# Program order pinned on every engine in a gated recurrence with a highway layer: gate and product two units ahead, decay one ahead, output one behind

## The chip, the cores and the metric

The kernel runs on one core of one Trainium2 chip. The metric is the device time of one launch in microseconds (us); lower is better. The engines named below: PE is TensorE (matmuls and transposes), DVE is VectorE, ACT is ScalarE, POOL is GpSimd, and SP is the sync engine, whose queue issues the large DMAs. "1024 KB" in a row is 1024 x 1024 bytes, 1.049 MB.

## The reference

For four sequences of 6336 steps and 256 channels a gated linear recurrence runs over time, and a highway layer is applied to its output:

```python
sig = 1 / (1 + exp(-f_logit))
f = lower_bound + (1 - lower_bound) * sig
h[t] = f[t] * h[t-1] + (1 - f[t]) * x[t]          # y[t] = h[t], per sequence and channel
H = maximum(y @ w_h, 0)
T = 1 / (1 + exp(-(y @ w_t + b_t)))
out = T * H + (1 - T) * y
```

Inputs and output are fp32; 1024 rows of 256 values are 1.049 MB.

## The kernel before

The work is cut into 25 units. Unit 0 holds the first 192 steps of all four sequences (768 rows); units 1 to 24 hold 1024 steps of one sequence each, in the order in which the four sequences take turns. The channels are two halves of 128, called h or m. With u = sigmoid(-f_logit) and c = 1 - lower_bound, the decay is f = 1 - c u, and the recurrence is run on b = u x and scaled by c later, so that `ncc` holds -c and the weights and diagonal matrices hold c already.

The steps of one unit, each a helper function of the kernel:

- `load` (line 65): two DMAs on SP's queue bring `lt` (f_logit) and `xt` (x), 128 partitions of eight rows each.
- `gate` (L114): ACT makes `u`, one instruction on the whole unit. `product` (L121): POOL makes `bv` = u x in four instructions.
- `decay_pe` (L128): PE transposes one half of `u`, eight blocks, into the PSUM tile `uT`; `decay_act` (L136): ACT makes the decay `f` from it. `b_pe` (L142): PE transposes one half of `bv` into `bT`.
- `scan` (L153): DVE runs the recurrence over 1024 steps for one half, from `f` and `bT`, into `y`. It starts from the last column of the same sequence, four units earlier.
- `z_pe` (L167), four matmuls into `zp`; `t_act` (L175), ACT's sigmoid `t`. `g_pe` (L181 and L184), six matmuls into `gp`; `d_dve` (L193), DVE's `d`; `e_dve` (L200), DVE's `e` = d t for both halves. z and g of either half need the scans of both halves.
- `o_pe` (L216, L217), called four times with q = 0 to 3: eight matmuls each turn a quarter of the unit back into rows, in `op`; `o_act` (L225): ACT copies the quarter to `o`; after the last quarter one DMA on SP's queue stores the unit (L229).

The PSUM tiles `uT`, `bT`, `zp` and `gp` have one buffer each, `op` has two. In SBUF, `lt` and `xt` have three buffers, `u`, `bv`, `f` and `e` three, `t`, `d` and `o` two, `y` six.

The loop at line 239 emits, in iteration n, steps of units n-2 to n+2: the scan of unit n, z, g, d, t and e of unit n-1, the output of unit n-2, gate, product and decay of unit n+1, and the load of unit n+2. This is the order of the program, but not the order on the engines: a scheduler at build time takes instructions as it expects them to become ready, the program's order being its priority, and fixes a sequence for each engine. At run time each engine and each queue works in that sequence. Buffers are handed on by semaphores: a tile's next user waits until all readers of its buffer are done.

Of the kernel before, what the change touches and what calls it, by code (L numbers as in the profile page):

```python
# [19 lines left out]
def kernel(  # L20
# [19 lines left out]
    P = 128  # L40
# [69 lines left out]

    def gate(n):
        np_, _ = units[n]
        u = mid.tile([P, NB, D], FP16, tag="u")
        nc.scalar.activation(u[:np_], st[n]["lt"][:np_], AF.Sigmoid, scale=-1.0)  # L114
        st[n]["u"] = u

    def product(n):
        np_, _ = units[n]
        bv = mid.tile([P, NB, D], BF16, tag="bv")
        for q in range(0, NB, 2):  # L120
            nc.gpsimd.tensor_mul(bv[:np_, q:q + 2], st[n]["u"][:np_, q:q + 2], st[n]["xt"][:np_, q:q + 2])  # L121
        st[n]["bv"] = bv

    def decay_pe(n, h):
        np_, _ = units[n]
        uT = ps1.tile([P, NB * P], FP16, tag="uT")
        for j in range(NB):
            nc.tensor.transpose(uT[:, j * np_:(j + 1) * np_], st[n]["u"][:np_, j, h * P:(h + 1) * P], ident_h[:np_, :np_])  # L128
        st[n]["uT"] = uT

    def decay_act(n, h):
        np_, _ = units[n]
        N = NB * np_
        if h == 0:
            st[n]["f"] = mid.tile([P, NH, NB * P], FP16, tag="f", name="f")
        nc.scalar.activation(st[n]["f"][:, h, :N], st[n]["uT"][:, :N], AF.Identity, scale=ncc[:, h:h + 1], bias=1.0)  # L136

    def b_pe(n, h):
        np_, _ = units[n]
        bT = ps1.tile([P, NB * P], BF16, tag="bT")  # L140
        for j in range(NB):
            nc.tensor.transpose(bT[:, j * np_:(j + 1) * np_], st[n]["bv"][:np_, j, h * P:(h + 1) * P], ident_b[:np_, :np_])  # L142
        st[n]["bT"] = bT

    carry = {}
# [1 line left out]
    def scan(n, h):  # L147
        if h == 0:
            st[n]["y"] = ypool.tile([P, NH, NB * P], BF16, tag="y", name="y")
        y = st[n]["y"]  # L150
        for b, _, c0, ln in units[n][1]:
            prev = carry.get((b, h))
            nc.vector.tensor_tensor_scan(  # L153
                y[:, h, c0:c0 + ln], st[n]["f"][:, h, c0:c0 + ln], st[n]["bT"][:, c0:c0 + ln],
                0.0 if prev is None else prev, op0=ALU.mult, op1=ALU.add)
            carry[b, h] = y[:, h, c0 + ln - 1:c0 + ln]

    def halves(n):
# [3 lines left out]
    def z_pe(n, m):  # L162
        zp = ps1.tile([P, 2, 512], FP32, tag="zp")
        y = st[n]["y"]
        for ki in range(NH):
            for i, (a, e) in enumerate(halves(n)):
                nc.tensor.matmul(zp[:, i, :e - a], w_sb[:, 1, ki, m * P:(m + 1) * P], y[:, ki, a:e],  # L167
                                 start=ki == 0, stop=ki == NH - 1)
        st[n]["zp"] = zp

    def t_act(n, m):
        w = NB * units[n][0] // 2
        if m == 0:
            st[n]["t"] = ffn.tile([P, NH, 2, 512], BF16, tag="t", name="t")
        nc.scalar.activation(st[n]["t"][:, m, :, :w], st[n]["zp"][:, :, :w], AF.Sigmoid, bias=bt[:, m:m + 1])  # L175

    def g_pe(n, m):
        gp = ps1.tile([P, 2, 512], FP32, tag="gp")
        y = st[n]["y"]
        for i, (a, e) in enumerate(halves(n)):  # L180
            nc.tensor.matmul(gp[:, i, :e - a], ndiag[:, m], y[:, m, a:e], start=True, stop=False)  # L181
        for ki in range(NH):
            for i, (a, e) in enumerate(halves(n)):
                nc.tensor.matmul(gp[:, i, :e - a], w_sb[:, 0, ki, m * P:(m + 1) * P], y[:, ki, a:e],  # L184
                                 start=False, stop=ki == NH - 1)
        st[n]["gp"] = gp

    def d_dve(n, m):
        w = NB * units[n][0] // 2
        if m == 0:  # L190
            st[n]["d"] = ffn.tile([P, NH, 2, 512], BF16, tag="d", name="d")
        y2 = st[n]["y"][:, m, :2 * w].rearrange("p (i w) -> p i w", i=2)
        nc.vector.scalar_tensor_tensor(st[n]["d"][:, m, :, :w], y2, ncc[:, m:m + 1], st[n]["gp"][:, :, :w],  # L193
                                       op0=ALU.mult, op1=ALU.max)

    def e_dve(n):
        w = NB * units[n][0] // 2
        e = mid.tile([P, NH, 2, 512], BF16, tag="e", name="e")
        if w == 512:
            nc.vector.tensor_mul(e, st[n]["d"], st[n]["t"])  # L200
        else:
            for m in range(NH):
                nc.vector.tensor_mul(e[:, m, :, :w], st[n]["d"][:, m, :, :w], st[n]["t"][:, m, :, :w])
        st[n]["e"] = e

    def o_pe(n, q):
        np_, _ = units[n]
        w = NB * np_ // 2
        op = ps2.tile([P, 2, D], FP32, tag="op")
        y, e = st[n]["y"], st[n]["e"]  # L210
        for jj in range(2):
            j = 2 * q + jj
            i, c = divmod(j * np_, w)
            for h in range(NH):
                o = op[:np_, jj, h * P:(h + 1) * P]
                nc.tensor.matmul(o, y[:, h, j * np_:(j + 1) * np_], diag[:, h], start=True, stop=False)  # L216
                nc.tensor.matmul(o, e[:, h, i, c:c + np_], ident_b, start=False, stop=True)  # L217
        st[n]["op"] = op

    def o_act(n, q):  # L220
        np_, segs = units[n]
# [13 lines left out]

    def ok(n):
        return 0 <= n < NU

    for n in range(-2, NU + 2):
        if ok(n + 2) and n + 2 > 1:  # L240
            load(n + 2)
        if ok(n):
            b_pe(n, 0)
            scan(n, 0)
        if ok(n - 1):
            g_pe(n - 1, 0)
# [11 lines left out]
        if ok(n):  # L258
            b_pe(n, 1)
            scan(n, 1)  # L260
        if ok(n + 1):
            decay_pe(n + 1, 0)
            decay_act(n + 1, 0)
        if ok(n - 1):
            g_pe(n - 1, 1)
            z_pe(n - 1, 1)
            d_dve(n - 1, 1)
            t_act(n - 1, 1)
        if ok(n + 1):
            decay_pe(n + 1, 1)  # L270
            decay_act(n + 1, 1)
        if ok(n - 1):
            e_dve(n - 1)
# [37 lines left out]
```

## Time and profile before

| | us |
|---|---|
| median of three runs | 317.29 |
| fastest and slowest of them | 313.27, 318.69 |
| the profiled execution, its whole time | 312.08 |
| its span, first to last instruction | 310.0 |

The rows below come from that one profiled execution, so sums are made against 312.08 and its span. Busy time is what an engine spent in instructions; a chain of waits is followed back from the last instruction to what released it at each step, and its shares are shares of the span. In a timeline row the first number is the start in us from the start of the span, the second the length, then engine, line, operation, tile written from tiles read, and shapes; "xN" merges N instructions of one kind that follow each other. What stands in square brackets is how long the engine had been idle and what ended it. Instructions of one engine may overlap a little at their ends, so the distance from start to start is often shorter than the length shown.

### The profile page before, as it was taken

Reading aid. Unit: us, or ns where it says so; the run is one execution under the profiler, and the core shown is the slowest. Engines: PE = TensorE matmul, PEld = TensorE weight load, DVE = VectorE, ACT = ScalarE, POOL = GpSimd, SP = SyncE. Lnnn points to the kernel's source line nnn. Section 1 sums busy time; section 2 is a strip of 40 time slices with the busy share of each in tenths; the row PEclk is TensorE's granted clock in tenths of the full one; section 3 lists DMA queues with packets and bytes.
Section 4 is the critical chain, followed back from the end, with each engine's and each line's share of the span. In section 5 each row is a group of like instructions: output and inputs, shape, how many; then the busy total and the mean of one; then the engine's idle time right before and its main releaser. Section 6 shows DMA issues by size and latency. Waiting matters only on the chain.

```text
span 310.0 us, 5042 instructions
## 1 busy us (share of the span) xinstructions
PE 222.9 (72%) x2100; PEld 145.1 (47%) x2100; DVE 207.8 (67%) x142; ACT 203.2 (66%) x226; POOL 120.0 (39%) x108
## 2 busy tenths in 40 slices
PE   0287789779696787876876967768578578578682
PEld 0154556546263554454453644545355345356451
DVE  0269899779586886595775674846956857847850
ACT  1356888696395755966757656757658657667552
POOL 1566452561543623514605235055054054153100
PEclk9999999999899999999979799799999999999798
DMA  7999149999969599699849588597796796733037
GB/s 188 335 386 385 62 121 350 378 341 309 289 218 320 180 316 332 232 323 334 253 163 333 179 295 278 203 330 228 252 331 185 270 333 190 253 137 135 2 135 271
DMA packets 78422, 78.70 MB, mean 254 GB/s; under 512 B 1856, under 2 KB 78400, under 8 KB 78400
## 3 DMA queue, kind: packets, MB, share of 16 engines
q1 hardware_dynamic: 77280, 77.86, 75.9%
q10 hardware_dynamic: 1120, 0.53, 0.7%
q8 instruction: 16, 0.26, 0.4%
q14 instruction: 6, 0.05, 0.0%
HBM read 52.43 MB, written 25.95 MB: 253 GB/s over the span
## 4 chain that ended last, share of the span: by engine, by line
POOL 29%; issue 27%; PE 15%; DVE 13%; ACT 6%; DMA 6%; SPq 1%; POOLq 1%; DVEq 0%; ACTq 0%
POOL bv L121 29%; DVE y L153 10%; DMA xt<-in_x_dram 5%; PE gp L184 4%; PE zp L167 4%; ACT u L114 3%; PE bT L142 3%; DVE d L193 2%; ACT o L225 2%; PE gp L181 1%; DMA lt<-in_f_logit_dram 1%; PE op L216 1%; ACT t L175 1%; PE op L217 1%; PE uT L128 1%
## 5 line engine op out<-in xcount | busy, mean ns | idle before, releaser
L121 POOL TENSOR_TENSOR bv<-u,xt 128x512 bf16<-128x512 f16 (+1 forms) x100 | 118.9, 1220 | 167.6 <-ACT u L114 131.3
L153 DVE TENSOR_TENSOR_SCAN y<-f,y,bT 128x1024 bf16<-128x1024 f16 x48 | 112.5, 2344 | 43.5 <-PE bT L142 37.6
L175 ACT ACTIVATE t<-zp,bt 128x1024 bf16<-128x1024 f32 (+1 forms) x50 | 55.2, 1104 | 51.2 <-PE zp L167 51.0
L193 DVE SCALAR_TENSOR_TENSOR d<-y,ncc,gp 128x1024 bf16<-128x1024 bf16 (+1 forms) x50 | 62.9, 1257 | 31.2 <-PE gp L184 31.2
L142 PE MATMUL bT<-ident_b,bv 128*128 128x128 bf16 (+1 forms) x400 | 43.1, 228 | 53.4 <-POOL bv L121 26.7
L136 ACT ACTIVATE f<-uT,ncc 128x1024 f16<-128x1024 f16 (+1 forms) x50 | 55.4, 1108 | 26.9 <-PE uT L128 26.2
L225 ACT COPY o<-op 128x512 f32<-128x512 f32 (+1 forms) x100 | 53.9, 590 | 16.2 <-PE op L217 15.2
L184 PE MATMUL gp<-y,w_sb 128*128 128x512 bf16 (+1 forms) x200 | 57.2, 384 | 9.9 <-DVE y L153 9.9
L142 PEld LDWEIGHTS <-bv 128*128 128x128 bf16 (+1 forms) x400 | 28.1, 101 | 74.5 <-POOL bv L121 36.9
L216 PE MATMUL op<-diag,y 128*128 128x128 f16 (+1 forms) x400 | 56.5, 228 | 2.1 <-ACT o L225 1.4
L167 PE MATMUL zp<-y,w_sb 128*128 128x512 bf16 (+1 forms) x200 | 56.1, 384 | 0.0
L217 PE MATMUL op<-ident_b,e 128*128 128x128 bf16 (+1 forms) x400 | 56.0, 227 | 0.1
L114 ACT ACTIVATE u<-lt 128x2048 f16<-128x2048 f32 (+1 forms) x25 | 47.9, 1918 | 0.6 <-DMA lt<-in_f_logit_dram 0.6
L216 PEld LDWEIGHTS <-y 128*128 128x128 bf16 (+1 forms) x400 | 41.4, 104 | 5.9 <-issue 1.6
L217 PEld LDWEIGHTS <-e 128*128 128x128 bf16 (+1 forms) x400 | 41.1, 103 | 6.4 <-issue 1.3
L128 PE MATMUL uT<-ident_h,u 128*128 128x128 f16 (+1 forms) x400 | 31.3, 223 | 11.3 <-ACT u L114 10.0
L181 PE MATMUL gp<-y,ndiag 128*128 128x512 bf16 (+1 forms) x100 | 32.4, 393 | 4.3 <-DVE d L193 4.0
L128 PEld LDWEIGHTS <-u 128*128 128x128 f16 (+1 forms) x400 | 25.9, 100 | 18.0 <-ACT u L114 11.0
L184 PEld LDWEIGHTS <-w_sb 128*128 128x128 bf16 x200 | 19.3, 99 | 30.5 <-issue 14.6
L200 DVE TENSOR_TENSOR e<-d,t 128x2048 bf16<-128x2048 bf16 x24 | 31.0, 1291 | 3.4 <-ACT t L175 2.9
L167 PEld LDWEIGHTS <-w_sb 128*128 128x128 bf16 x200 | 19.4, 99 | 19.6 <-issue 2.0
L181 PEld LDWEIGHTS <-ndiag 128*128 128x128 f16 x100 | 8.9, 103 | 3.9 <-issue 3.9
(16 smaller groups left out, 10.3 us busy)
## 6 DMA issues: line engine op xcount, KB each, us to landing
lt<-in_f_logit_dram SPq DMA_DIRECT2D x24, 1024.0 KB, 8.0
xt<-in_x_dram SPq DMA_DIRECT2D x24, 1024.0 KB, 9.7
out_dram<-o SPq DMA_DIRECT2D x24, 1024.0 KB, 5.3
lt<-in_f_logit_dram SPq DMA_DIRECT2D x2, 384.0 KB, 5.0
xt<-in_x_dram SPq DMA_DIRECT2D x2, 384.0 KB, 5.7
out_dram<-o SPq DMA_DIRECT2D x2, 384.0 KB, 5.0
w_raw<-in_moe_w_h_dram ACTq DMA_DIRECT2D x1, 256.0 KB, 4.8
w_raw<-in_moe_w_t_dram ACTq DMA_DIRECT2D x1, 256.0 KB, 5.3
```

Of the source, the lines that this page charges most:

```text
L114: nc.scalar.activation(u[:np_], st[n]["lt"][:np_], AF.Sigmoid, scale=-1.0)
L121: nc.gpsimd.tensor_mul(bv[:np_, q:q + 2], st[n]["u"][:np_, q:q + 2], st[n]["xt"][:np_, q:q + 2])
L128: nc.tensor.transpose(uT[:, j * np_:(j + 1) * np_], st[n]["u"][:np_, j, h * P:(h + 1) * P], ident_h[:np_, :np_])
L142: nc.tensor.transpose(bT[:, j * np_:(j + 1) * np_], st[n]["bv"][:np_, j, h * P:(h + 1) * P], ident_b[:np_, :np_])
L153: nc.vector.tensor_tensor_scan(y[:, h, c0:c0 + ln], st[n]["f"][:, h, c0:c0 + ln], st[n]["bT"][:, c0:c0 + ln], 0.0 if prev is None else pre ...
L167: nc.tensor.matmul(zp[:, i, :e - a], w_sb[:, 1, ki, m * P:(m + 1) * P], y[:, ki, a:e], start=ki == 0, stop=ki == NH - 1)
L175: nc.scalar.activation(st[n]["t"][:, m, :, :w], st[n]["zp"][:, :, :w], AF.Sigmoid, bias=bt[:, m:m + 1])
L184: nc.tensor.matmul(gp[:, i, :e - a], w_sb[:, 0, ki, m * P:(m + 1) * P], y[:, ki, a:e], start=False, stop=ki == NH - 1)
L193: nc.vector.scalar_tensor_tensor(st[n]["d"][:, m, :, :w], y2, ncc[:, m:m + 1], st[n]["gp"][:, :, :w], op0=ALU.mult, op1=ALU.max)
L216: nc.tensor.matmul(o, y[:, h, j * np_:(j + 1) * np_], diag[:, h], start=True, stop=False)
L217: nc.tensor.matmul(o, e[:, h, i, c:c + np_], ident_b, start=False, stop=True)
L225: nc.scalar.copy(o[:np_, 2 * q:2 * q + 2], st[n]["op"][:np_])
```

## The change

Every instruction of the loop, save the loads of unit 0, the stores and the set-up, goes through `pin`, which keeps the pinned instructions of an engine in the order of the program. The order itself is new: the loads run four units ahead (two before), gate and product two ahead (one before), the decay one ahead as before, and with it b_pe of the first half; z, g, d, t and e stay one behind, save that g of the first half moves to the end of the scan's own iteration; the output stays two iterations behind the scan. The pool of `lt` and `xt` gets a fourth buffer, and `u` moves into it from the pool with three. The store is split: half a unit after the second quarter and half after the fourth.

```diff
-    inp = ctx.enter_context(tc.tile_pool(name="inp", bufs=3))
+    inp = ctx.enter_context(tc.tile_pool(name="inp", bufs=4))
...
+    def pin(ins):
+        return tc.keep_in_program_order(ins)
...
-                nc.sync.dma_start(t, src[b, s0:s0 + ln, :].rearrange("(j p) d -> p j d", p=np_))
+                pin(nc.sync.dma_start(t, src[b, s0:s0 + ln, :].rearrange("(j p) d -> p j d", p=np_)))
...
-        u = mid.tile([P, NB, D], FP16, tag="u")
-        nc.scalar.activation(u[:np_], st[n]["lt"][:np_], AF.Sigmoid, scale=-1.0)
+        u = inp.tile([P, NB, D], FP16, tag="u")
+        pin(nc.scalar.activation(u[:np_], st[n]["lt"][:np_], AF.Sigmoid, scale=-1.0))
...
-        nc.scalar.copy(o[:np_, 2 * q:2 * q + 2], st[n]["op"][:np_])
+        pin(nc.scalar.copy(o[:np_, 2 * q:2 * q + 2], st[n]["op"][:np_]))
+        if len(segs) == 1 and q % 2 == 1:
+            b, s0, _, ln = segs[0]
+            a = s0 + (q // 2) * (ln // 2)
+            nc.sync.dma_start(out_bsd[b, a:a + ln // 2, :].rearrange("(j p) d -> p j d", p=np_),
+                              o[:, 2 * q - 2:2 * q + 2])
...
-    for n in range(-2, NU + 2):
-        if ok(n + 2) and n + 2 > 1:
-            load(n + 2)
+    for n in range(-3, NU + 2):
+        if ok(n + 4) and n + 4 > 1:
+            load(n + 4)
+        if ok(n - 1):
+            z_pe(n - 1, 0)
         if ok(n):
-            b_pe(n, 0)
             scan(n, 0)
...
```

The other instructions are wrapped in `pin` in the same way. The loop after the change, in the order in which it emits (the conditions `ok(...)` are left out):

```python
for n in range(-3, NU + 2):
    load(n + 4)
    z_pe(n - 1, 0); scan(n, 0); t_act(n - 1, 0)
    o_pe(n - 2, 0); o_act(n - 2, 0); o_pe(n - 2, 1); o_act(n - 2, 1)
    decay_pe(n + 1, 0); decay_act(n + 1, 0)
    d_dve(n - 1, 0); b_pe(n, 1)
    z_pe(n - 1, 1); t_act(n - 1, 1)
    scan(n, 1); g_pe(n - 1, 1)
    gate(n + 2); product(n + 2)
    o_pe(n - 2, 2); o_act(n - 2, 2); o_pe(n - 2, 3); o_act(n - 2, 3)
    b_pe(n + 1, 0); decay_pe(n + 1, 1); decay_act(n + 1, 1)
    d_dve(n - 1, 1); e_dve(n - 1); g_pe(n, 0)
```

## Rows read from the trace of the kernel before

**Rows 1.** The page, busy us (share of the span) and instructions of each engine.

```profile
PE 222.9 (72%) x2100; PEld 145.1 (47%) x2100; DVE 207.8 (67%) x142; ACT 203.2 (66%) x226; POOL 120.0 (39%) x108
```

**Rows 2.** The page, chain that ended last, share of the span by engine.

```profile
POOL 29%; issue 27%; PE 15%; DVE 13%; ACT 6%; DMA 6%; SPq 1%; POOLq 1%; DVEq 0%; ACTq 0%
```

**Rows 3.** Timeline of all engines, one period late in the run (248 to 262 us).

```profile
248.10 4.51 POOL L121 TENSOR_TENSOR bv<-u,xt 128x512 bf16<-128x512 f16 x4 [7.12 <-ACT u L114]
...
253.07 2.35 DVE L153 TENSOR_TENSOR_SCAN y<-f,y,bT 128x1024 bf16<-128x1024 f16 x1 [3.73 <-PE bT L142]
...
256.33 1.11 ACT L175 ACTIVATE t<-zp,bt 128x1024 bf16<-128x1024 f32 x1 [2.52 <-PE zp L167]
...
257.34 1.06 ACT L225 COPY o<-op 128x512 f32<-128x512 f32 x2
...
258.29 1.93 ACT L114 ACTIVATE u<-lt 128x2048 f16<-128x2048 f32 x1
...
260.29 2.28 POOL L121 TENSOR_TENSOR bv<-u,xt 128x512 bf16<-128x512 f16 x2 [7.67 <-ACT u L114]
```

**Rows 4.** Timeline of DVE, four instructions that follow each other without a gap.

```profile
145.60 1.26 DVE L193 SCALAR_TENSOR_TENSOR d<-y,ncc,gp 128x1024 bf16<-128x1024 bf16 x1
146.77 2.34 DVE L153 TENSOR_TENSOR_SCAN y<-f,y,bT 128x1024 bf16<-128x1024 f16 x1
149.03 1.20 DVE L200 TENSOR_TENSOR e<-d,t 128x2048 bf16<-128x2048 bf16 x1
150.14 1.27 DVE L193 SCALAR_TENSOR_TENSOR d<-y,ncc,gp 128x1024 bf16<-128x1024 bf16 x1
```

**Rows 5.** Timeline of ACT, four rows that follow each other without a gap.

```profile
124.20 1.90 ACT L114 ACTIVATE u<-lt 128x2048 f16<-128x2048 f32 x1
126.00 1.06 ACT L225 COPY o<-op 128x512 f32<-128x512 f32 x2
126.94 1.14 ACT L136 ACTIVATE f<-uT,ncc 128x1024 f16<-128x1024 f16 x1
127.95 1.13 ACT L175 ACTIVATE t<-zp,bt 128x1024 bf16<-128x1024 f32 x1
```

**Rows 6.** Timeline of PE, a stretch without a gap (sixteen output matmuls from 50.58 on).

```profile
47.97 0.61 PE L142 MATMUL bT<-ident_b,bv 128*128 128x128 bf16 x8
48.42 0.59 PE L181 MATMUL gp<-y,ndiag 128*128 128x512 bf16 x2
...
49.71 1.03 PE L167 MATMUL zp<-y,w_sb 128*128 128x512 bf16 x4
50.58 0.22 PE L216 MATMUL op<-diag,y 128*128 128x128 f16 x1
...
51.41 0.22 PE L217 MATMUL op<-ident_b,e 128*128 128x128 bf16 x1
```

**Rows 7.** Timeline of DVE, first scans of units 1, 3 and 4, second of 24.

```profile
23.77 2.35 DVE L153 TENSOR_TENSOR_SCAN y<-f,y,bT 128x1024 bf16<-128x1024 f16 x1
...
40.47 2.33 DVE L153 TENSOR_TENSOR_SCAN y<-f,y,bT 128x1024 bf16<-128x1024 f16 x1
...
49.12 2.34 DVE L153 TENSOR_TENSOR_SCAN y<-f,y,bT 128x1024 bf16<-128x1024 f16 x1
...
292.27 2.35 DVE L153 TENSOR_TENSOR_SCAN y<-f,y,bT 128x1024 bf16<-128x1024 f16 x1
```

**Rows 8.** Windows: length, busy PE, PEld, DVE, ACT, POOL, clock, DMA share, GB/s.

```profile
48.00:68.00 20.00, 17.03 (x177) 11.43 (x174) 16.99 (x11) 16.46 (x19) 9.16 (x8) 1.00 1.08 377
...
211.25:220.75 9.50, 6.54 (x66) 4.27 (x66) 6.83 (x6) 6.38 (x7) 4.83 (x4) 1.00 1.01 331
```

**Rows 9.** The tile e on DVE: duration ns shortest/median/longest, first and last start.

```profile
L200 DVE TENSOR_TENSOR e<-d,t x24: 1197/1201/2046, 38.6 to 300.5; 128x2048 bf16<-128x2048 bf16 x24
```

**Rows 10.** The page, granted TensorE clock in 40 slices, tenths of full speed.

```profile
PEclk9999999999899999999979799799999999999798
```

More of the change, by code (lines that the diff above doesn't have):

```diff
@@ L127, in decay_pe @@
         for j in range(NB):
-            nc.tensor.transpose(uT[:, j * np_:(j + 1) * np_], st[n]["u"][:np_, j, h * P:(h + 1) * P], ident_h[:np_, :np_])
+            pin(nc.tensor.transpose(uT[:, j * np_:(j + 1) * np_], st[n]["u"][:np_, j, h * P:(h + 1) * P], ident_h[:np_, :np_]))
         st[n]["uT"] = uT
@@ L141, in b_pe @@
         for j in range(NB):
-            nc.tensor.transpose(bT[:, j * np_:(j + 1) * np_], st[n]["bv"][:np_, j, h * P:(h + 1) * P], ident_b[:np_, :np_])
+            pin(nc.tensor.transpose(bT[:, j * np_:(j + 1) * np_], st[n]["bv"][:np_, j, h * P:(h + 1) * P], ident_b[:np_, :np_]))
         st[n]["bT"] = bT
@@ L152, in scan @@
             prev = carry.get((b, h))
-            nc.vector.tensor_tensor_scan(
+            pin(nc.vector.tensor_tensor_scan(
                 y[:, h, c0:c0 + ln], st[n]["f"][:, h, c0:c0 + ln], st[n]["bT"][:, c0:c0 + ln],
-                0.0 if prev is None else prev, op0=ALU.mult, op1=ALU.add)
+                0.0 if prev is None else prev, op0=ALU.mult, op1=ALU.add))
             carry[b, h] = y[:, h, c0 + ln - 1:c0 + ln]
@@ L166, in z_pe @@
             for i, (a, e) in enumerate(halves(n)):
-                nc.tensor.matmul(zp[:, i, :e - a], w_sb[:, 1, ki, m * P:(m + 1) * P], y[:, ki, a:e],
-                                 start=ki == 0, stop=ki == NH - 1)
+                pin(nc.tensor.matmul(zp[:, i, :e - a], w_sb[:, 1, ki, m * P:(m + 1) * P], y[:, ki, a:e],
+                                 start=ki == 0, stop=ki == NH - 1))
         st[n]["zp"] = zp
@@ L180, in g_pe @@
         for i, (a, e) in enumerate(halves(n)):
-            nc.tensor.matmul(gp[:, i, :e - a], ndiag[:, m], y[:, m, a:e], start=True, stop=False)
+            pin(nc.tensor.matmul(gp[:, i, :e - a], ndiag[:, m], y[:, m, a:e], start=True, stop=False))
         for ki in range(NH):
             for i, (a, e) in enumerate(halves(n)):
-                nc.tensor.matmul(gp[:, i, :e - a], w_sb[:, 0, ki, m * P:(m + 1) * P], y[:, ki, a:e],
-                                 start=False, stop=ki == NH - 1)
+                pin(nc.tensor.matmul(gp[:, i, :e - a], w_sb[:, 0, ki, m * P:(m + 1) * P], y[:, ki, a:e],
+                                 start=False, stop=ki == NH - 1))
         st[n]["gp"] = gp
@@ L215, in o_pe @@
                 o = op[:np_, jj, h * P:(h + 1) * P]
-                nc.tensor.matmul(o, y[:, h, j * np_:(j + 1) * np_], diag[:, h], start=True, stop=False)
-                nc.tensor.matmul(o, e[:, h, i, c:c + np_], ident_b, start=False, stop=True)
+                pin(nc.tensor.matmul(o, y[:, h, j * np_:(j + 1) * np_], diag[:, h], start=True, stop=False))
+                pin(nc.tensor.matmul(o, e[:, h, i, c:c + np_], ident_b, start=False, stop=True))
         st[n]["op"] = op
@@ L257 @@
             o_act(n - 2, 1)
-        if ok(n):
-            b_pe(n, 1)
-            scan(n, 1)
         if ok(n + 1):
@@ L264 @@
         if ok(n - 1):
-            g_pe(n - 1, 1)
[L266 to L273, printed above, removed]
+            d_dve(n - 1, 0)
+        if ok(n):
+            b_pe(n, 1)
+        if ok(n - 1):
+            z_pe(n - 1, 1)
+            t_act(n - 1, 1)
+        if ok(n):
+            scan(n, 1)
+        if ok(n - 1):
+            g_pe(n - 1, 1)
+        if ok(n + 2):
+            gate(n + 2)
+            product(n + 2)
         if ok(n - 2):
@@ L278 @@
             o_act(n - 2, 3)
+        if ok(n + 1):
+            b_pe(n + 1, 0)
+            decay_pe(n + 1, 1)
+            decay_act(n + 1, 1)
+        if ok(n - 1):
+            d_dve(n - 1, 1)
+            e_dve(n - 1)
+        if ok(n):
+            g_pe(n, 0)
         if ok(n - 2):
```

25 lines of the change are left out of this document (8 added, 17 removed).

## Prediction

> **What bounds the kernel now.** I first read the busy times: no engine fills the span. VectorE (DVE) is busy 207.8 us of 310.0 and GpSimd (POOL) only 120.0 [rows 1]. Yet the chain of work that ended last runs through POOL more than through any other engine: 29%, with 27% more in waits that the profile cannot name [rows 2]. An engine that is 39% busy and still leads the chain is a link in a loop, so I went to the timeline of one period late in the run [rows 3] to find the loop. There the reader sees it close: the products of a unit start on POOL at 248.10 and take 4.51; the scan of that unit, which had waited 3.73 for its transposes, starts at 253.07; ScalarE (ACT) can make t only at 256.33, after waiting 2.52 for PE; the output copies follow at 257.34, the gate of the next unit at 258.29, and its products at 260.29. That is 12.19 us from product to product. In words: product, transpose, scan, matmul, t, output copy, gate, product. The gate stands in ACT's queue behind copies that belong to older units, so the one engine that feeds the next scan starts late each time.
>
> How long a unit takes on average: the first full-size scan starts at 23.77 and the last one, of unit 24, at 292.27 and runs 2.35 [rows 7]. I count a unit from its first scan to the next unit's, so I add the one d and the one e that follow the second scan (1.17 + 1.11, below): 24 units in 292.27 + 2.35 + 2.3 - 23.77 = 273.2, or 11.4 each. What is left behind is 310.0 - 296.9 = 13.1 of tail. So span = 23.8 + 24 x period + 13.1.
>
> **The floors of one unit**, from starts to starts where an engine had no gap (instructions overlap a little at their ends, so these are shorter than durations). DVE: d 145.60 to 146.77 is 1.17, scan to 149.03 is 2.26, e to 150.14 is 1.11 [rows 4]; two scans, two d and one e make 2 x 2.26 + 2 x 1.17 + 1.11 = 7.97. ACT: gate 1.80, two copies 0.94, f 1.01 [rows 5], t 1.01 [rows 3]; one gate, four copies, two f, two t make 1.80 + 1.88 + 2.02 + 2.02 = 7.72. PE: eight transposes 0.45, the six matmuls of g 1.29, the four of z 0.87, sixteen output matmuls from 50.58 to the start of the last at 51.41, 0.055 apart, so 0.89 [rows 6]; four transpose groups, two g, two z, and 32 output matmuls make 1.80 + 2.58 + 1.74 + 1.78 = 7.90. POOL: 4.51 [rows 3]. DMA: two loads and one store of 1024 rows x 256 x 4 bytes = 3.15 MB; with the queue never empty it moved 377 GB/s over 20 us, stores among the loads, which is 8.35 per unit; in a burst that begins on an idle queue it moved 331 over 9.5 us, which is the same 3.15 MB in 9.5 [rows 8]. Four resources lie between 7.7 and 8.4, and the period is 11.4: there are 3 us of waiting per unit to win, and little beyond.
>
> **The change, part by part.**
>
> *Gate and product two units ahead.* The same instructions move: no new work. The product of unit n+2 is made in iteration n and read by b_pe(n+2,0) at the end of iteration n+1, so it has some 1.4 periods for 4.51 of work. The loop above is opened at POOL; this takes POOL off the chain. The cover is the fourth input buffer and u's move to that pool; without them the gate would wait for a slot.
>
> *Fourth input buffer, loads four ahead.* The slot of load n+4 is free when product n ends, early in iteration n-1, and gate(n+4) reads it in iteration n+2: over two periods of slack for the load. Cost nothing, hidden by that slack, as long as DMA keeps up per unit. Stores in halves: one more issue on the sync queue per unit, same bytes. Stores are not pinned, so the sync queue's order between stores and loads is the scheduler's; that slack covers a load behind a store. Where it is gone, the gate is late next, and everything behind it on ACT.
>
> *The pinned order.* I walk one iteration, 0 at scan(n,0), by the starts above. DVE: scan(n,0) at 0, d(n-1,0) at 2.26, scan(n,1) at 3.43, d(n-1,1) at 5.69, e at 6.86, next scan at 7.97. PE begins with z(n-1,0) at 0.3, because g(n-1,0) ahead of it waited for d of the iteration before (that ends near 7.0 of the frame before). Two output groups 1.2 to 2.1, transposes of u to 2.5, b_pe(n,1) to 3.0 with its result in time for 3.43, z(n-1,1) to 3.8, g(n-1,1) to 5.1, in time for 5.69. Output groups to 6.0, b_pe(n+1,0) to 6.5, in time for 7.97, transposes to 6.9, then g(n,0) waits for d(n-1,1) and ends at 8.3: back at the start, 7.97 later. ACT: t at 1.4, copies 2.4, f 3.4, t 4.4, gate 5.4, copies 7.2, f 8.1, next t at 9.1, where z is ready at 9.4. Every DVE wait for PE is covered by another DVE operation (b_pe(n,1) by d, g by scan, b_pe(n+1,0) by d and e). Behind each waiting PE group stands the rest of PE's queue, so lateness is passed on, and PE has 0.07 of air per period. Nothing in the order needs more than the DVE floor: lower bound of the period 8.0.
>
> *From floor to period.* Hand-overs are not free and four resources at 7.7 to 8.4 will not fit without gaps. The nearest row is a stretch of the kernel before in which its products were ready early: from scan to scan of the next unit 40.47 to 49.12, 8.65 [rows 7]. Both kernels run the same work there, with the loop of POOL absent. It also clears the DMA floor of 8.35. I take 8.6. The lower bound is 8.0 (DVE), the upper the burst figure, 9.5.
>
> *The product beside e.* In the walk gate(n+2) ends near 7.3 and e runs 6.86 to 8.0: products begin just as e runs, every iteration, where now they mostly miss each other. e usually takes 1.20 but up to 2.05 [rows 9]. I price this at nothing, because e is issued first in the walk and POOL has over 3 us of air to absorb its own wait. The margin is 0.4 us; if it is gone, 0.85 per unit. The Trainium skill, SBUF — State Buffer, section "Who interferes with whom", says that a VectorE instruction with two SBUF inputs contends with a GpSimd one that reads SBUF, and that issue order decides who waits. By that rule e pays in the unlucky order; the trace's 1.20 to 2.05 agrees that such a price exists.
>
> *Start and tail.* The first loads and the first unit's work are the same; 23.8 stays, within 2 either way (a gate is 1.8). The tail after the last scan is unit 24's own work, which the new order does not shorten; 13.1 stays.
>
> **Sum.** 23.8 + 24 x 8.6 + 13.1 = 243.3 of span. The profiled execution took 312.08 for a span of 310.0, so add 2.1: 245.4. The median of the runs is 317.29, 1.017 times that execution; 245.4 x 1.017 = 249.5, and I write 249. The same steps give 235 at period 8.0, 257 at 8.9, 271 at 9.5.
>
> **Rivals.**
>
> *DMA sets the pace.* At 8.6 it would be 97% occupied. If two half-stores per unit bring back the weak stretches that a burst on an idle queue shows, the period is 9.5 and the time 271. For it: 331 against 377 GB/s [rows 8]. Against it: the weak stretches were seen after idle queues, and this queue will rarely idle. The Trainium skill, HBM Reference, section "Specifications (TRN2)", gives about 358 GB/s as a core's share, which would make an estimated 8.8 per unit and 254 by the sum; the trace's 377 over 20 us is above it.
>
> *e pays for POOL.* Period 8.6 + 0.85 = 9.45, time 270.
>
> *Covers gone.* If PE's in-order queue falls so far behind that DVE waits out b_pe(n,1) and both g in full, 0.45 + 1.29 + 1.29, the period is 8.0 + 3.0 = 11.0 and the time 308, hardly a gain. For it: PE has next to no air. Against: in the walk each has 0.2 to 1.3 us in hand, and in the 8.65 stretch PE was as full.
>
> *Slower: PE at its low clock.* PE is now nearly a full engine, so its clock becomes a price. In four of forty slices of the run before the granted clock is only 7 tenths, a mix of 2.4 and 1.2 GHz [rows 10]. With a share s of the work at 1.2 GHz, PE needs 7.9 x (1 + s); beyond 11.4, so from s = 0.45, the kernel is slower than before; all of it at 1.2 GHz gives a period of 15.8 and 425. Against: 34 of the forty slices stand at 9, with PE busy much as it will be.
>
> *Nothing changes.* If the scheduler's order was already close to this one, the time stays near 317. Against: in [rows 3] the gate follows the copies of older units.
>
> **Chances.** Period 8.0 to 8.9, 235 to 257: 0.62. DMA pace, 257 to 271: 0.17. e pays, about 270: 0.10. Covers gone in part or in full, 285 to 310: 0.06, a sixth of it within 2%. Slower by the clock: 0.03. No change: 0.02. So faster by over 2% 0.94, within 2% (what a measurement of this kernel can hardly tell from no change) 0.03, slower 0.03. The range takes in the first three: 234 to 274.
>
> **What the profile after would show.** Right: scan(n,0) to scan(n+1,0) near 8.6; POOL's products starting one iteration before their transposes and gone from the chain; DVE busy some 85% of its span; DMA rarely idle. DMA rival: gates waiting for lt, GB/s near 340 with a full queue. e rival: e near 2.0 on average. Covers: long waits of scans for bT and d for gp. Clock: granted clock well under 0.9. I would be wrong most easily on the period: 0.1 us in it is 2.4 us.

## The result and the profile after

The change makes the kernel faster: 252.55 us median (252.02 to 257.77) against 316.44 for the kernel before, a ratio of 0.8005 with an interval of 0.7939 to 0.807. The forecast was 249 in 234 to 274.

| | before | after |
|---|---|---|
| median | 316.44 us | 252.55 us |
| profiled execution, its span | 312.08, 310.0 us | 257.77, 256.0 us |
| VectorE busy | 207.8 us, 67% | 223.0 us, 87% |
| GpSimd busy | 120.0 us, 39% | 135.4 us, 53% |
| GpSimd's share of the last chain | 29% | none named |

The profiled execution of the changed kernel, with a span of 256.0, is one of its longer ones; the shorter ones have spans of 250.2 to 251.0 and no profile. Line numbers after are three higher than before.

The page of the changed kernel: busy us of each engine, then the chain that ended last, by engine and by line (answering [rows 1] and [rows 2]).

```profile
PE 211.5 (83%) x2100; PEld 142.8 (56%) x2100; DVE 223.0 (87%) x142; ACT 201.5 (79%) x226; POOL 135.4 (53%) x108
...
DVE 77%; PE 6%; issue 5%; ACT 2%; DVEq 0%; ACTq 0%
DVE y L156 41%; DVE e L203 18%; DVE d L196 17%; PE zp L170 2%; PE gp L187 1%; PE bT L145 1%; ACT u L117 1%; PE uT L131 1%; ACT o L228 1%; PE gp L184 1%; DVE e L206 1%; PE op L220 0%; PE op L219 0%; ACT t L178 0%; DVEq L203 0%
```

GpSimd, first in the chain before, is out of it: VectorE's own work, one instruction after the other, is 77% of the chain. But two busy times grew although the instructions are the same: VectorE by 15 us and GpSimd by 15. The tile view says which VectorE instruction grew (answering [rows 9]; duration in ns shortest/median/longest, first and last start).

```profile
L203 DVE TENSOR_TENSOR e<-d,t x24: 1224/2142/2147, 40.4 to 247.1; 128x2048 bf16<-128x2048 bf16 x24
```

Before, the median e took 1201 ns; now it is 2142. Timeline of all engines of the changed kernel, one period late in the run (start, duration, engine, line, operation, wait before it; answering [rows 3]).

```profile
206.40 2.33 DVE L156 TENSOR_TENSOR_SCAN y<-f,y,bT 128x1024 bf16<-128x1024 f16 x1
...
208.78 0.61 PE L145 MATMUL bT<-ident_b,bv 128*128 128x128 bf16 x8 [0.79 <-DVE y L156]
209.23 1.03 PE L170 MATMUL zp<-y,w_sb 128*128 128x512 bf16 x4
...
210.29 1.11 ACT L178 ACTIVATE t<-zp,bt 128x1024 bf16<-128x1024 f32 x1 [0.56 <-PE zp L170]
...
211.31 1.90 ACT L117 ACTIVATE u<-lt 128x2048 f16<-128x2048 f32 x1
212.08 1.25 DVE L196 SCALAR_TENSOR_TENSOR d<-y,ncc,gp 128x1024 bf16<-128x1024 bf16 x1
...
213.34 5.51 POOL L124 TENSOR_TENSOR bv<-u,xt 128x512 bf16<-128x512 f16 x4 [3.60 <-issue]
...
213.44 2.14 DVE L203 TENSOR_TENSOR e<-d,t 128x2048 bf16<-128x2048 bf16 x1
...
215.50 2.33 DVE L156 TENSOR_TENSOR_SCAN y<-f,y,bT 128x1024 bf16<-128x1024 f16 x1
```

From scan to scan is 9.10 us where it was about 12, and no VectorE row has a wait behind it (of the later units only one does: its e stood idle for 0.51 us). The product starts 0.10 us ahead of e, and both are about 1 us longer than in [rows 3] and [rows 4]. The timeline of POOL alone, cut behind the first and behind the second of the four products, shows where GpSimd lost its part.

```profile
213.34 1.16 POOL L124 TENSOR_TENSOR bv<-u,xt 128x512 bf16<-128x512 f16 x1 [3.60 <-issue]
...
213.34 3.27 POOL L124 TENSOR_TENSOR bv<-u,xt 128x512 bf16<-128x512 f16 x2 [3.60 <-issue]
```

The first product ends at 214.50, the second only at 216.61, 2.11 later. e, issued at 213.44, ends at 215.58. So e stands behind the first product for about 1 us, then the second product stands behind e for about 1 us. That this always falls out the same way is in the period above: the transposes wait for the first scan, z stands behind the transposes in TensorE's queue, t waits for z, the gate stands behind t on ScalarE, and the product needs the gate. Product and e are thus both timed from the same scan (213.34 is 6.94 behind it, 213.44 is 7.04), and a longer e cannot pull them apart. The kernel is locked into the bad order.

Timeline of VectorE of the changed kernel, its last periods, where one e meets no product.

```profile
222.54 2.14 DVE L203 TENSOR_TENSOR e<-d,t 128x2048 bf16<-128x2048 bf16 x1
224.61 2.33 DVE L156 TENSOR_TENSOR_SCAN y<-f,y,bT 128x1024 bf16<-128x1024 f16 x1
...
231.65 1.22 DVE L203 TENSOR_TENSOR e<-d,t 128x2048 bf16<-128x2048 bf16 x1
232.79 2.34 DVE L156 TENSOR_TENSOR_SCAN y<-f,y,bT 128x1024 bf16<-128x1024 f16 x1
```

Here nothing is left to multiply on GpSimd, e takes 1.22 again, and the period is 8.18. The lock costs 0.92 us in each unit.

### The profile page after: what moved, and what is told of

Same layout as the page of the kernel before. It is cut to its first block, busy times and chain, and to the rows that moved or that the text cites. A ratio compares the mean times of both kernels' runs of the same rounds, so it can differ in the third digit from the quotient of the medians.

```text
span 256.0 us, 5101 instructions
## 1 busy us (share of the span) xinstructions
PE 211.5 (83%) x2100; PEld 142.8 (56%) x2100; DVE 223.0 (87%) x142; ACT 201.5 (79%) x226; POOL 135.4 (53%) x108
## 4 chain that ended last, share of the span: by engine, by line
DVE 77%; PE 6%; issue 5%; ACT 2%; DVEq 0%; ACTq 0%
DVE y L156 41%; DVE e L203 18%; DVE d L196 17%; PE zp L170 2%; PE gp L187 1%; PE bT L145 1%; ACT u L117 1%; PE uT L131 1%; ACT o L228 1%; PE gp L184 1%; DVE e L206 1%; PE op L220 0%; PE op L219 0%; ACT t L178 0%; DVEq L203 0%
## 5 line engine op out<-in xcount | busy, mean ns | idle before, releaser
L124 POOL TENSOR_TENSOR bv<-u,xt 128x512 bf16<-128x512 f16 (+1 forms) x100 | 134.3, 1373 | 92.0 <-issue 75.5
L145 PE MATMUL bT<-ident_b,bv 128*128 128x128 bf16 (+1 forms) x400 | 31.9, 223 | 24.8 <-DVE y L156 20.6
L219 PE MATMUL op<-diag,y 128*128 128x128 f16 (+1 forms) x400 | 52.0, 221 | 0.5 <-ACT o L228 0.5
L220 PE MATMUL op<-ident_b,e 128*128 128x128 bf16 (+1 forms) x400 | 51.1, 221 | 1.4 <-DVE e L203 1.4
L170 PE MATMUL zp<-y,w_sb 128*128 128x512 bf16 (+1 forms) x200 | 51.6, 381 | 0.3 <-ACT t L178 0.3
L187 PE MATMUL gp<-y,w_sb 128*128 128x512 bf16 (+1 forms) x200 | 51.5, 381 | 0.0
L203 DVE TENSOR_TENSOR e<-d,t 128x2048 bf16<-128x2048 bf16 x24 | 48.3, 2011 | 2.9 <-ACT o L228 0.5
L220 PEld LDWEIGHTS <-e 128*128 128x128 bf16 (+1 forms) x400 | 39.2, 100 | 9.8 <-DVE e L203 6.3
L145 PEld LDWEIGHTS <-bv 128*128 128x128 bf16 (+1 forms) x400 | 26.1, 100 | 28.9 <-issue 21.5
L184 PE MATMUL gp<-y,ndiag 128*128 128x512 bf16 (+1 forms) x100 | 29.8, 380 | 2.0 <-DVE d L196 0.9
## 6 DMA issues: line engine op xcount, KB each, us to landing
w_raw<-in_moe_w_h_dram ACTq DMA_DIRECT2D x1, 256.0 KB, 4.8
w_raw<-in_moe_w_t_dram ACTq DMA_DIRECT2D x1, 256.0 KB, 5.4
```

What stands on the lines that cost most here:

```text
L124: pin(nc.gpsimd.tensor_mul(bv[:np_, q:q + 2], st[n]["u"][:np_, q:q + 2], st[n]["xt"][:np_, q:q + 2]))
L145: pin(nc.tensor.transpose(bT[:, j * np_:(j + 1) * np_], st[n]["bv"][:np_, j, h * P:(h + 1) * P], ident_b[:np_, :np_]))
L170: pin(nc.tensor.matmul(zp[:, i, :e - a], w_sb[:, 1, ki, m * P:(m + 1) * P], y[:, ki, a:e], start=ki == 0, stop=ki == NH - 1))
L187: pin(nc.tensor.matmul(gp[:, i, :e - a], w_sb[:, 0, ki, m * P:(m + 1) * P], y[:, ki, a:e], start=False, stop=ki == NH - 1))
L203: pin(nc.vector.tensor_mul(e, st[n]["d"], st[n]["t"]))
L219: pin(nc.tensor.matmul(o, y[:, h, j * np_:(j + 1) * np_], diag[:, h], start=True, stop=False))
```

## Experiments

All ratios are to the kernel before, run on the same chip in the same series.

**1. Move the gate and the product behind e.** Theory: the product's start just ahead of e costs 0.9 us per unit.

```diff
-        if ok(n + 2):
-            gate(n + 2)
-            product(n + 2)
...
+        if ok(n + 2):
+            gate(n + 2)
+            product(n + 2)
```

The three lines go from the middle of the iteration to behind its last two output copies.

> The gate of unit n+2 stands behind the last two output copies on ACT instead of ahead of them; nothing else moves. In the changed kernel the products start 0.10 us ahead of e in every period, and e takes 2.14 us instead of 1.20. Theory A (e waits for the first product on POOL, and DVE is the pace): the products now start about 1 us after e has, e falls to about 1.2, POOL waits for e instead; the period falls from 9.11 to 8.2 (as in the last period of the changed kernel, which has no product beside e and lasts 8.18) or to the DMA floor of 8.35, so 231 to 238 us. Rival B (DMA sets the pace near 9.1 and e's length only fills the wait): e shorter, but scans wait, period near 9.0, time 249 to 253. Rival C (the gate now comes too late for ACT): period over 9.3, time over 257.

Measured: 235.95 us, ratio 0.7591 (0.7535 to 0.7646). Timeline of all engines, one period, then the tile e, then a window of 8 us (busy PE, PEld, DVE, ACT, POOL, clock, DMA share, GB/s; answering [rows 8]).

```profile
200.83 1.26 DVE L196 SCALAR_TENSOR_TENSOR d<-y,ncc,gp 128x1024 bf16<-128x1024 bf16 x1
...
201.74 1.92 ACT L117 ACTIVATE u<-lt 128x2048 f16<-128x2048 f32 x1
202.19 1.23 DVE L203 TENSOR_TENSOR e<-d,t 128x2048 bf16<-128x2048 bf16 x1
203.33 2.34 DVE L156 TENSOR_TENSOR_SCAN y<-f,y,bT 128x1024 bf16<-128x1024 f16 x1
203.80 4.53 POOL L124 TENSOR_TENSOR bv<-u,xt 128x512 bf16<-128x512 f16 x4 [3.65 <-issue]
...
211.52 2.34 DVE L156 TENSOR_TENSOR_SCAN y<-f,y,bT 128x1024 bf16<-128x1024 f16 x1
```

```profile
L203 DVE TENSOR_TENSOR e<-d,t x24: 1225/1225/1228, 38.0 to 225.8; 128x2048 bf16<-128x2048 bf16 x24
```

```profile
150.00:158.00 8.00, 7.89 (x84) 5.53 (x84) 7.89 (x6) 7.68 (x10) 4.33 (x4) 1.00 1.09 384
```

The product now starts behind e's end (202.19 + 1.23 = 203.42), every e takes 1.225, the product 4.53, the period is 8.19. PE, VectorE and ScalarE are each busy over 95% of the window, at 384 GB/s. Theory held.

**2. Hold the product alone.** Moving the gate also moves work on ScalarE. Here ScalarE, VectorE and TensorE keep their orders; GpSimd first copies one column of e, and so waits for it.

```diff
+            if ok(n - 1):
+                hold = mid.tile([P, 1], BF16, tag="hold", name="hold")
+                pin(nc.gpsimd.tensor_copy(hold, st[n - 1]["e"][:, 1, 1, :1]))
             product(n + 2)
```

> A copy of one column of e on POOL, ahead of the products of unit n+2, holds them until e of unit n-1 is done; ACT's, PE's and DVE's orders are those of the changed kernel. Theory A: e near 1.2, period 8.2 to 8.45, time 231 to 239, as with the gate moved. If the gate's place on ACT, and not POOL beside e, is what costs, this kernel stays at 250 to 253 while the one with the gate moved falls. Rival B (DMA): 249 to 253.

Measured: 237.87 us, ratio 0.7647 (0.7598 to 0.7695). Timeline of all engines, one period.

```profile
152.37 1.94 ACT L117 ACTIVATE u<-lt 128x2048 f16<-128x2048 f32 x1
154.36 1.23 DVE L203 TENSOR_TENSOR e<-d,t 128x2048 bf16<-128x2048 bf16 x1
155.50 2.34 DVE L156 TENSOR_TENSOR_SCAN y<-f,y,bT 128x1024 bf16<-128x1024 f16 x1
155.65 0.19 POOL L289 COPY hold<-e 128x1 bf16<-128x1 bf16 x1 [3.52 <-DVE e L203]
```

The gate ends at 154.31 and e starts at 154.36: without the hold the two would meet again. GpSimd's wait costs nothing, it has 3.5 us of air; the period is 8.22 (147.28 to 155.50). So it is the order of product and e that cost 0.9, not the gate's place on ScalarE.

**3. The same depth without the pin.**

```diff
     def pin(ins):
-        return tc.keep_in_program_order(ins)
+        return ins
```

> The new order of the program, its depth, its four buffers and its split store, but nothing pinned: the scheduler takes the order on each engine. Theory D (the depth opens the loop, the pinning only keeps the order): gates run ahead, 245 to 262 us. Rival E (the pinning is what the gain hangs on, since the scheduler puts the gate behind older copies again): 285 to 317 us.

Measured: 305.67 us, ratio 0.9823 (0.9759 to 0.9887). Two rows of the waits (engine, line, waited for: us in total, times, longest), then the timeline.

```profile
POOL bv L124 <- issue: 129.8, 22, 9.2
...
DVE y L156 <- PE bT L145: 42.2, 24, 6.6
```

```profile
156.13 5.50 POOL L124 TENSOR_TENSOR bv<-u,xt 128x512 bf16<-128x512 f16 x4 [7.60 <-issue]
...
162.08 2.35 DVE L156 TENSOR_TENSOR_SCAN y<-f,y,bT 128x1024 bf16<-128x1024 f16 x1 [2.59 <-PE bT L145]
```

The loops are written two units ahead, but the product again comes just before its own scan (156.13, scan at 162.08), as in [rows 3]. The rival held: the depth as written carries next to nothing, because the scheduler undoes it.

**4. The old order and depth, pinned.** The kernel before, with every instruction kept in the order in which it is written.

```diff
-        nc.scalar.activation(u[:np_], st[n]["lt"][:np_], AF.Sigmoid, scale=-1.0)
+        pin(nc.scalar.activation(u[:np_], st[n]["lt"][:np_], AF.Sigmoid, scale=-1.0))
...
```

> The kernel before with every instruction of its loop pinned in the order of its own program, its old depth, three buffers, one store per unit. Theory D: the loop gate, product, transposes, scan, z, t, gate stays closed inside one unit (about 2.3 + 0.5 + 1.3 + 1.1 + 1.0 + 1.9 + 4.5 + 0.7 us), so a period near 11 to 13 and 290 to 340 us. Rival F (any fixed order would have done it): under 275 us.

Measured: 281.25 us, ratio 0.9056 (0.8981 to 0.913), between the two expectations, so both numbers missed. Its waits:

```profile
POOL bv L124 <- ACT u L117: 129.8, 23, 8.2
```

GpSimd still waits for the gate, 5.6 us per unit, and leads the chain with 36%: product and gate still close a loop, but not quite that of [rows 3]. The scans no longer wait for their transposes; the transposes, which need the product (151.66 to 156.18), hold up the z behind them in TensorE's queue, and with it t (158.72) and the gate (159.73). The period is 10.05, since the written order has the gate ahead of the output copies. So the pin without the depth takes 9.4% off the time and the depth without the pin 1.8%, where both together take 20%.

**5. Three buffers, and the changed kernel once more.** Input buffers back to three, u back in its pool; beside it the changed kernel itself.

```diff
-    inp = ctx.enter_context(tc.tile_pool(name="inp", bufs=4))
+    inp = ctx.enter_context(tc.tile_pool(name="inp", bufs=3))
...
-        u = inp.tile([P, NB, D], FP16, tag="u")
+        u = mid.tile([P, NB, D], FP16, tag="u")
```

> The changed kernel with lt, xt and u in three buffers as before; order and pinning unchanged. A load can then be issued only when the products of the unit three earlier are done, some 2 periods (18 us) ahead of its gate; loads took about 8 to 11 us to land. Theory G (the fourth buffer carries nothing once the order is right): 250 to 256 us. Rival H (the fourth buffer is needed for the depth): gates wait for lt, over 262 us.

> The changed kernel itself once more, for its time beside the other kernels of this call and for a second profile. Every theory: 251 to 254 us, period 9.1 from first scan to first scan, e near 2.14, products starting about 0.1 us ahead of e.

Measured: 252.55 us, ratio 0.8071 (0.8 to 0.8141) with three buffers; 257.42, ratio 0.8209 (0.8129 to 0.8289) for the changed kernel. The changed kernel missed its 251 to 254 us this time, though its profile shows what was expected (period 9.11, e 2.144 in the median, the product at 40.68 and e at 40.78). With three buffers it is no slower, so the fourth carries nothing that is seen here. Timelines of VectorE and of GpSimd of the kernel with three buffers, in order of time, e and product of five units in a row.

```profile
38.00 1.23 DVE L203 TENSOR_TENSOR e<-d,t 128x2048 bf16<-128x2048 bf16 x1
...
38.46 5.15 POOL L124 TENSOR_TENSOR bv<-u,xt 128x512 bf16<-128x512 f16 x4 [3.04 <-ACT u L117]
...
46.19 1.23 DVE L203 TENSOR_TENSOR e<-d,t 128x2048 bf16<-128x2048 bf16 x1
...
46.37 5.44 POOL L124 TENSOR_TENSOR bv<-u,xt 128x512 bf16<-128x512 f16 x4 [2.76 <-ACT u L117]
...
54.38 1.23 DVE L203 TENSOR_TENSOR e<-d,t 128x2048 bf16<-128x2048 bf16 x1
...
54.47 5.52 POOL L124 TENSOR_TENSOR bv<-u,xt 128x512 bf16<-128x512 f16 x4 [2.66 <-ACT u L117]
...
62.66 5.51 POOL L124 TENSOR_TENSOR bv<-u,xt 128x512 bf16<-128x512 f16 x4 [2.67 <-ACT u L117]
62.97 1.93 DVE L203 TENSOR_TENSOR e<-d,t 128x2048 bf16<-128x2048 bf16 x1 [0.51 <-ACT u L117]
...
71.71 4.38 POOL L124 TENSOR_TENSOR bv<-u,xt 128x512 bf16<-128x512 f16 x3 [3.54 <-ACT u L117]
...
71.86 2.09 DVE L203 TENSOR_TENSOR e<-d,t 128x2048 bf16<-128x2048 bf16 x1
```

In the first three units e is issued first: it keeps its 1.23 and only the product pays. But e's lead shrinks, 0.46, 0.18, 0.09, because the product comes 7.91 and 8.10 us behind the last one (38.46, 46.37, 54.47) and e every 8.19: the gate's side has slack and drifts forward. It is not the drift that turns the order: the next product comes 8.19 behind (62.66), which would have left e its 0.09. This time e is late: VectorE stands idle for 0.51, and e starts at 62.97 where 54.38 + 8.19 = 62.57 was due. The product is first, and from then on it stays so. The same idle 0.51 to 0.54, ahead of the fourth of the full-size e, stands in the profiles of the changed kernel and of experiments 1, 2 and 6 as well; what it waits for is not shown, since the profiles name three different instructions. Where product and e stand well apart (experiment 1) or are held apart (experiment 2), it costs only itself. In both profiles of the changed kernel the lock was there from the first full unit, at spans of 256.0 and 256.4; here it set in after three, at 249.4.

**6. One store per unit.**

```diff
-        if len(segs) == 1 and q % 2 == 1:
...
-                              o[:, 2 * q - 2:2 * q + 2])
...
+            if len(segs) == 1:
+                b, s0, _, ln = segs[0]
+                nc.sync.dma_start(out_bsd[b, s0:s0 + ln, :].rearrange("(j p) d -> p j d", p=np_), o)
```

> The changed kernel with one store per unit, after the last quarter, as before. The last unit's first half is then stored later: 1 to 2 us at the very end. Theory G (DVE paces, stores are behind it): 252 to 256 us. Rival H (o has two buffers, and a whole store lands too late, so copies wait on ACT): over 259 us.

Measured: 254.26 us, ratio 0.8128 (0.8055 to 0.8201): not told apart from the changed kernel. The halves carry nothing that can be seen here.

**7. Late gate, and e in two halves.** In experiment 1 VectorE is the floor, and e starts 1.36 behind its d (200.83 to 202.19) where a scan starts 1.17 behind one: it reads what that d has just written. Halves let e begin with the older d.

```diff
-        if w == 512:
-            pin(nc.vector.tensor_mul(e, st[n]["d"], st[n]["t"]))
-        else:
-            for m in range(NH):
-                pin(nc.vector.tensor_mul(e[:, m, :, :w], st[n]["d"][:, m, :, :w], st[n]["t"][:, m, :, :w]))
+        for m in range(NH):
+            pin(nc.vector.tensor_mul(e[:, m, :, :w], st[n]["d"][:, m, :, :w], st[n]["t"][:, m, :, :w]))
```

> The kernel with the gate behind the last copies, and e made in two halves, of which the first reads a d that has long been written. In the kernel with the gate late, e starts 1.36 us after the d ahead of it, where instructions that read nothing just written follow d after 1.17; its period is 8.19, DVE is at work in 7.9 of every 8 us, and DMA moves 384 GB/s, which is 8.19 per unit too. Theory A (DVE is the pace): the wait of 0.19 falls away and a second instruction costs up to 0.1, so a period of 8.0 to 8.1 and 232 to 235 us. Rival B (DMA is at its floor as well): period stays 8.19, DVE waits where it had none, 235.5 to 237 us.

Measured: 234.54 us (232.61 to 235.19), ratio 0.7482 (0.7417 to 0.7547), the fastest kernel of the study. Its interval and that of experiment 1 overlap a little, so its own gain over that one, about 1%, is likely and not shown. Windows of 40 us:

```profile
100.00:140.00 40.00, 39.56 (x413) 27.72 (x419) 40.00 (x31) 39.08 (x45) 22.34 (x21) 1.00 1.09 382
```

Its period is 8.06 early in the run (30.88 to 38.94) and 8.17 later (151.81 to 159.98). Early, the first half of e starts 1.17 behind the d ahead of it, as a scan does, so it is the reading of what was just written that cost the 0.19:

```profile
44.63 1.26 DVE L196 SCALAR_TENSOR_TENSOR d<-y,ncc,gp 128x1024 bf16<-128x1024 bf16 x1
45.80 1.29 DVE L203 TENSOR_TENSOR e<-d,t 128x1024 bf16<-128x1024 bf16 x2
```

Later, the waits have a row that experiment 1 has not; its seven waits all lie behind 145 us:

```profile
ACT o L225 <- DMA out_dram<-o: 3.1, 7, 1.0
```

The output copy waits for a store to leave its buffer.

**8. The same with half of the stores.** Do transfers make the 8.06 into 8.17? This kernel leaves out the second store of each full-size unit, so half of their output is never written.

```diff
-        if len(segs) == 1 and q % 2 == 1:
+        if len(segs) == 1 and q == 1:
```

> The version with the late gate and e in halves, with the second half of every one-segment unit's output left unstored (that half of the result is missing; all computing is done). A quarter of the loop's traffic goes. Theory F, the transfers set the last tenths of that version's period (379 to 382 GB/s, period 8.17 us late against 8.06 early): the period falls to 8.00 to 8.06 us everywhere and the time to 228 to 232 us. Rival G, the engines are at their own floor (DVE 40.00 us busy of 40, PE 39.55): the period stays 8.15 to 8.19 us and the time 232.5 to 235.5 us.

Measured: 232.73 us, ratio 0.7427 (0.7355 to 0.7498); the same window:

```profile
100.00:140.00 40.00, 39.94 (x420) 27.64 (x419) 40.00 (x31) 39.09 (x46) 22.34 (x21) 1.00 1.00 327
```

The period stays 8.06 (147.11 to 155.17), and no output copy waits for a store: in experiment 7 it is the transfers that add the 0.1 late in the run. The times do not show the gain: the median lies in the rival's span, and the intervals overlap. What it shows for the forecast: taking a quarter of the bytes away moves the period by 0.1 at most. At 8.06 the transfers just begin to be the bound; at the changed kernel's 9.1 they are not.

**9 to 11. Which engine's order carries the depth?** The changed kernel with the pin on one engine alone.

```diff
+    def keep(ins):
+        return ins
...
-            pin(nc.gpsimd.tensor_mul(bv[:np_, q:q + 2], st[n]["u"][:np_, q:q + 2], st[n]["xt"][:np_, q:q + 2]))
+            keep(nc.gpsimd.tensor_mul(bv[:np_, q:q + 2], st[n]["u"][:np_, q:q + 2], st[n]["xt"][:np_, q:q + 2]))
...
```

> The changed kernel's loops, buffers and stores with the order held on ScalarE alone; the other engines' orders are left to the scheduler. Theory H, the gate's place on ScalarE is what the scheduler undoes: with it held the product is again a whole unit early, the period is 8.5 to 9.5 us and the time 240 to 265 us. Rival I, the orders of the other engines (the scans and d/e on VectorE, transposes and matmuls on TensorE) matter as much: 280 to 306 us.

> The changed kernel's loops, buffers and stores with the order held on TensorE alone. Theory H (the gate's place on ScalarE is what counts): the gate still comes just in time, 285 to 310 us. Rival I: the transposes and matmuls held in their places pull the gate and the product forward with them, 245 to 280 us.

> The changed kernel's loops, buffers and stores with the order held on VectorE alone. Held on TensorE alone it took 250.7 us, on ScalarE alone 274.1, on none 305.7. Theory J, it is TensorE's queue that carries the depth, because the transposes of a later unit stand there among the matmuls of earlier ones: held on VectorE alone the scans still wait for their transposes, 285 to 306 us. Rival K, any one engine that works on several units at once carries it: 248 to 275 us.

The last column is the start of unit 15's product against the start of that unit's first scan, in the traces.

| pinned | us | ratio (interval) | product ahead of its scan |
|---|---|---|---|
| none (3) | 305.67 | 0.9823 (0.9759 to 0.9887) | 162.08 - 156.13 = 5.95 us |
| VectorE | 304.71 | 0.9789 (0.968 to 0.9898) | 159.73 - 153.77 = 5.96 |
| ScalarE | 274.07 | 0.8732 (0.8666 to 0.8799) | 160.16 - 151.02 = 9.14 |
| TensorE | 250.73 | 0.8 (0.7936 to 0.8065) | 149.59 - 135.09 = 14.50 |
| all | 252.55 | 0.8005 (0.7939 to 0.807) | 151.76 - 140.49 = 11.27 |

The row of all engines is the changed kernel's first result; its second was 257.42 (0.8209). VectorE's order alone does nothing: the product comes as late as with no pin. ScalarE's order does bring the gate and the product forward, but takes only 12.7% off, between the two expectations. TensorE's order alone brings them forward and gives as much as all orders together, so the theory that the gate's place on ScalarE is what counts fell. Waits, of VectorE pinned:

```profile
DVE y L159 <- PE bT L148: 38.5, 23, 6.9
```

and of ScalarE pinned, with its tile e:

```profile
DVE d L199 <- PE gp L190: 26.5, 23, 2.5
...
L206 DVE TENSOR_TENSOR e<-d,t x24: 1198/1992/1998, 42.6 to 264.4; 128x2048 bf16<-128x2048 bf16 x24
```

In both, VectorE waits for TensorE in nearly every unit: for the transposes of a late product in the one, for g in the other, where the product is early and TensorE's order is not right. With ScalarE pinned e also meets the product in most units: it takes 1.99 in the median, so of its period of 10.02 about 0.8 goes to the same collision, beside 1.13 of waiting for g. With TensorE pinned, timeline of all engines:

```profile
157.15 1.23 DVE L206 TENSOR_TENSOR e<-d,t 128x2048 bf16<-128x2048 bf16 x1
158.29 2.34 DVE L159 TENSOR_TENSOR_SCAN y<-f,y,bT 128x1024 bf16<-128x1024 f16 x1
159.15 1.90 ACT L120 ACTIVATE u<-lt 128x2048 f16<-128x2048 f32 x1
161.18 4.53 POOL L127 TENSOR_TENSOR bv<-u,xt 128x512 bf16<-128x512 f16 x4 [4.16 <-issue]
162.15 2.35 DVE L159 TENSOR_TENSOR_SCAN y<-f,y,bT 128x1024 bf16<-128x1024 f16 x1 [0.34 <-ACT t L181]
```

The scheduler, left to order the other engines around it, gives VectorE the same order as the full pin, but puts the gate well behind e (159.15 against 157.15). So e takes 1.23 and the product 4.53: no lock. It loses elsewhere: ahead of one of the two scans VectorE stands idle for 0.34 in nearly every unit, the chain runs through ScalarE (34%) and TensorE (32%), and the period is 8.70 (153.45 to 162.15); the first full scan starts at 26.59 instead of 22.87. That this comes out at the time of the full pin is a coincidence. How the scheduler chooses was not tried.

## Why the prediction was right, and where it was not

**The loop opened at GpSimd: right.** The chain lost its 29%, and behind the first units no scan waits for its product. The forecast put this down to the depth, with the pin as the way to write it. Experiments 3 and 4 show that neither does it alone, and 9 to 11 that of the orders TensorE's is enough. It also said that without the fourth buffer the gate would wait for a slot; in experiment 5 it does not.

**Start and tail: close.** The first full scan starts at 22.87, forecast 23.8; behind unit 24 (232.79 + 8.19 = 240.98) remain 15.0 of span, forecast 13.1. Together they were 1.0 too low.

**From floor to period: over-sized.** The forecast added 0.6 to the floor of 7.97, taking 8.6 from a stretch of the kernel before. Where the lock is off (experiment 1) the pipeline ran at 8.19, all four resources filled. The 0.2 that is left is no hand-over between engines either: e starts 1.36 behind the d that it reads, and not 1.17 as the floor had it, and ends into the scan 1.14 later instead of 1.11. 7.97 + 0.19 + 0.03 = 8.19. The 8.65 stretch was too loose a model: both kernels run the same work in it, but not in the same order.

**The product beside e: priced at nothing, cost 0.92.** This is the step that failed. The walk put the gate's end at 7.3 behind the scan and e at 6.86, so that e would be issued first with 0.4 to spare. Measured, the gate ends at 6.81 (211.31 + 1.90 - 206.40) and e starts at 7.04: e is later by the d that it reads, and ScalarE is earlier, because in a period longer than its work it does not carry over the lateness that the walk gave it (its first t at 1.4 in the walk, its second at 4.4; measured 206.64 and 210.29, so 0.24 and 3.89). The product starts 0.13 behind the gate's end: e's margin was not 0.4 but minus 0.1. Out of the lock it was hardly better: in experiment 2 the gate ends 7.03 and e starts 7.08 behind the scan at 147.28, and in experiment 5 e led by 0.09 before one late start turned the order. The size that the rival gave, 0.85 per unit, was close to the 0.92 measured, and so was its mechanism. The Trainium skill, SBUF — State Buffer, section "Who interferes with whom", lets the order of issue decide who waits; the trace agrees on both sides of it: e first keeps 1.23 (38.00 in experiment 5), product first makes it 2.14. The forecast quoted that rule and then trusted a margin of 0.4 us, out of a walk whose steps were off by as much as 1.2.

**The sum.** Its form holds: with the numbers of the profiled execution, 22.9 + 24 x 9.09 + 15.0 = 256.0, where 9.09 is (240.98 - 22.87) / 24. The forecast had 8.6 for the period: too much by 0.41 for the hand-overs, too little by 0.92 for e. So two terms missed in opposite directions, and that the first made up for nearly half of the second is luck. Another part of the good agreement comes from the factor 1.017, the median of the kernel before over its profiled execution; after, that ratio is 252.55 / 257.77 = 0.98. The factor belongs to the kernel it was taken from. Without it the forecast is 245.4, and 7 too low. So the time fell into the likeliest case's span, for the reason of the third case on a lower base.

**DMA sets the pace: wrong, and the floor of 8.35 with it.** Loads and stores together moved 384 GB/s in experiment 1, more than the 377 of [rows 8], at a period below 8.35; and in the waits after, the gate waits for a load once, for 2.1 us, at the start. Where the transfers do begin to show is at 8.06 to 8.17 (experiments 7 and 8). Buffers and half-stores, costed at nothing, are worth nothing that was measured (experiments 5 and 6).

**Covers gone, and TensorE's clock: did not happen.** VectorE has one wait in the loop, of 0.51 us. The little air that TensorE has was enough even without the lock: in experiment 1 it is busy 7.89 of 8.00, and between the first units and the last no VectorE row waits for it. The granted clock was 1.00 in the windows shown, 0.987 on average in the profiled execution of the changed kernel.

**Nothing changes: did not happen**, but experiment 3 shows what stood between: written without the pin, the same loops give 305.67.

## What to carry to other kernels

When you pipeline deeper under a scheduler, look in the trace whether the early work really runs early; here holding TensorE's order was enough, the queue that carries the transposes of a later unit among the matmuls of older ones; VectorE's alone gave no more than no pin, ScalarE's alone a part, and GpSimd's and the loads' alone were not tried. When a floor is reached, list which instructions of VectorE and GpSimd will run beside each other and which is issued first: a start 0.1 us too early cost 0.92 us of 9.1 in each unit, and three lines moved gave it back. A margin from a hand-made walk is worth no more than the walk's largest error, and an order that rests on 0.1 us is turned for the rest of the run by one late start.

## What the runs showed of the hardware

The collision locks itself: a GpSimd multiply issued 0.10 us ahead of VectorE's e makes e 2.14 instead of 1.22 and the four products 5.51 instead of 4.53, and both are timed from one scan, so it repeats to the end; with three buffers the kernel started outside the lock and fell into it when e was late once, by 0.40 (experiment 5). VectorE's e, which reads the tile that the d before it has just written, starts 1.36 behind it; a scan, or a half of e that reads the older d, starts 1.17 behind (experiments 1 and 7). One core moved 384 GB/s with loads and stores mixed while three engines were over 95% busy.
